# A SwiGLU block behind linear attention: the first chunk's output product by seven half-block products, one batch's projections and scores two slots later, and the closing additions in another order

## The chip, the cores and the metric

One core of one Trainium2 chip. The metric is the device time of one execution in microseconds (us). Time before: a median of 554.39 us over three runs, 553.97 to 556.33.

## What is computed

For each of 8 batches and 8 heads, keys and values of 1024 rows are first projected to 64 rows by E and F; the attention over these 64 rows gives 8192 rows of 512 numbers; a feed-forward block with gate and value weights of 512 x 1536 and output weights of 1536 x 512 follows.

```python
def _attn_ref(q, k, v, E, F):
    k_proj = np.einsum('ks,bhsd->bhkd', E, k)
    v_proj = np.einsum('ks,bhsd->bhkd', F, v)
    scale = 1.0 / np.sqrt(q.shape[-1])
    scores = scale * np.matmul(q, k_proj.transpose(0, 1, 3, 2))
    scores = scores - np.max(scores, axis=-1, keepdims=True)
    attn = np.exp(scores)
    attn = attn / (np.sum(attn, axis=-1, keepdims=True) + 1e-09)
    return np.matmul(attn, v_proj).astype(np.float32)

def _moe_ref(x, w_gate, w_val, w_out):
    g = x @ w_gate
    silu = g * (1.0 / (1.0 + np.exp(-g)))
    val = x @ w_val
    return (silu * val @ w_out).astype(np.float32)
```

## The kernel before

The 8192 rows are cut into 16 chunks of 512 rows, two for each batch: chunk c belongs to batch c // 2. The outer loop (L849 to L858) runs over 192 steps; step t does column tile f = t mod 12 (128 of the 1536) of chunk c = t // 12. In each step `f_g` (L471) makes the gate product, four TensorE products of 512 columns over the four tiles of 128 inputs, and a tanh on ACT (L474); `f_v` (L477) makes the value product in the same way, and DVE multiplies gate, tanh and value together in two instructions (L481 and L486) into `hT`, the chunk's hidden values. Gate and value have two PSUM banks each.

The attention of later batches is placed by hand in between. A step has two slots: slot 2t lies between the gate and the value product, slot 2t + 1 at the end. `place` (L651) says in which slot each piece of a batch runs: `u_KV` (projections of keys and values), `u_KT` (the projected keys turned, and copied into the block-diagonal tile BD by four DVE copies), `u_TD` (queries turned by a DMA transpose on the SP queue, tile qTd), `u_S` (scores, eight groups, with an exp on ACT), `u_R` (row sums and reciprocals on DVE, the softmax pair), `u_N` (the normalised weights AA on POOL), `u_AD` (AA turned by a DMA transpose on SP, tile AT), `u_PV` (the attention's output, tile xT, which the gate and value products read). Batch 0's own second chunk is attended to in slots 12 to 22 (L803 to L812), with transposes on TensorE. Loads of k, v and q go out from POOL's queue, in slots of their own (L817 to L823). Batches are counted from 0: the third batch is b = 2.

The output product of a chunk runs one chunk later, from the list `late` (L829 to L847), which is worked off in each step between the value product and slot 2t + 1. There are two ways of doing it:

- Chunk 0 before: `f_y` (L492), the plain product. Twelve parts of four 512-column products each; for each 128 rows one PSUM bank, one ACT copy (L507) and one store (L508).
- Chunks 1 to 15: `f_m` (L604), one level of a seven-product scheme. Rows, columns and inner length are halved, and seven products of half size stand for eight. Their operands are sums of quarters: of the weights once (`w_sum`, L517, five sums ws1, ws3, ws4, ws6, ws7 on DVE), of the hidden values for each chunk (`h_sum`, L530: hs5 and hs2 tile by tile on POOL, hs1, hs6 and hs7 whole on DVE). Each product is six 256-column TensorE products (`m_mm`, L554), for each of two halves p of 128 rows: 14 groups for a chunk, in the order 3, 4, 5, 2, 1, 6, 7. Products 3 and 4 lie in a bank "y", are copied by ACT and added on POOL (`m_34`); products 5 and 2 are then added on top in the same bank and copied (`m_52`); products 1 and 6 lie in a bank "z". `m_16` (L590) adds product 1 on DVE (L593) and subtracts on POOL (L594); product 7 is then added on top of product 1 in its half bank, and `m_7` (L596) makes the last add on DVE (L599) and stores (L600) from SP.

Small products of the attention take banks of the kind "a" (two), and in the first two chunks also the bank "z" as a third in turn (`ring["wide"]`, L143 and L851). The tiles of hs5, hs2, hs1, hs6, hs7 also hold the first batch's turned queries and its weights AA (`first_batch`, L308).

The last chunk has its output product at the end (`f_m_last`, L616): the seven products, and for each p three DVE additions (L633 to L635) that make two partial sums; then product 7 and product 1 are made in one half bank, each followed by a DVE add (L640) and a store (L641) from SP or ACT's queue. Product 1 is added on top of product 7, so it must wait for product 7's L640.

The instructions of every engine run in the order in which the program gives them.

Of the kernel before, what the change touches and what calls it, by code (L numbers as in the profile page):

```python
# [10 lines left out]
ALU = mybir.AluOpType  # L11
AX = mybir.AxisListType
BF16 = mybir.dt.bfloat16
FP32 = mybir.dt.float32
# [6 lines left out]
DM = H * D  # L21
DFF = 1536
P = 128
# [3 lines left out]
NFT = DFF // P  # L27
# [3 lines left out]
NC = B * CH  # L31
# [7 lines left out]
def kernel(  # L39
# [19 lines left out]
    nc = tc.nc  # L59
# [10 lines left out]
    y_pool = ctx.enter_context(tc.tile_pool(name="ysb", bufs=2))  # L70
# [18 lines left out]
    wo = w_pool.tile([P, NFT, DM], BF16, name="wo")  # L89
    ws = {m: w_pool.tile([P, HF, HC], BF16, name=f"ws{m}") for m in (1, 3, 4, 6, 7)}  # L90

    kb, vb, qb, xT, hT = {}, {}, {}, {}, {}
# [47 lines left out]
    ring = {"n": 0, "wide": True}  # L140

    def bank(where, shape, dt, name):
        if where == "a" and ring["wide"]:  # L143
            where = "aaz"[ring["n"] % 3]
            ring["n"] += 1
        pool, tag = banks[where]
        return pool.tile(shape, dt, name=name, tag=tag)
# [323 lines left out]
    def f_g(c, f, i=None):  # L471
        ps = f_mm(c, f, 0, i)
        th = fw.tile([P, CW], FP32, name="th", tag="th")
        nc.scalar.activation(out=th[:], in_=ps[:], func=AF.Tanh, scale=0.5)  # L474
        gp[0] = (ps, th)
# [11 lines left out]
            out=hT[c][:, f, :], in0=s1[:], scalar=0.5, in1=ps[:], op0=ALU.mult, op1=ALU.mult  # L487
        )

    yy = {}  # L490

    def f_y(c, n):  # L492

        i, part = divmod(n, 3)
        if part == 0:
            yy[c] = bank("y", [P, DM], FP32, "yps")
        for f in range(4 * part, 4 * part + 4):
            nc.tensor.matmul(
                out=yy[c][:],
                lhsT=hT[c][:, f, i * P : (i + 1) * P],  # L500
                rhs=wo[:, f, :],
                start=(f == 0),
                stop=(f == NFT - 1),
            )
        if part == 2:
            ysb = y_pool.tile([P, 2, DM], FP32, name="ysb", tag="ysb")
            nc.scalar.copy(out=ysb[:, 0], in_=yy[c][:])  # L507
            nc.sync.dma_start(out=rows_of(c)[:, i, :], in_=ysb[:, 0])  # L508

    def rows_of(c):  # L510
        b, ch = divmod(c, CH)
        return out[b * S : (b + 1) * S, :].rearrange("(p c j) d -> p c j d", c=CH, j=4)[:, ch]
# [41 lines left out]
    def m_mm(c, p, m, ps, start=False):  # L554

        for f in range(HF):
            if m == 3:
                lhsT = hT[c][:, f, p * P : (p + 1) * P]
            elif m == 4:
                lhsT = hT[c][:, HF + f, HT + p * P : HT + (p + 1) * P]  # L560
            else:
                lhsT = hs[c, m][:, f, p * P : (p + 1) * P]
            rhs = {2: wo[:, f, 0:HC], 5: wo[:, HF + f, HC:DM]}.get(m)
            nc.tensor.matmul(  # L564
                out=ps,
                lhsT=lhsT,
                rhs=ws[m][:, f, :] if rhs is None else rhs,
                start=(start and f == 0),
                stop=(f == HF - 1),
                skip_group_check=True,  # L570
            )

    xx, zz, tt, yo = {}, {}, {}, {}

    def m_bank(at):
        return bank(at, [P, 2, HC], FP32, "yps")

    def m_34(c, p):

        xs = d_pool.tile([P, 2, HC], FP32, name="xs", tag="d")  # L580
        nc.scalar.copy(out=xs[:], in_=xx[c, p][:])  # L581
        t = tt[c, p] = d_pool.tile([P, 2, HC], FP32, name="tt", tag="t")
        nc.gpsimd.tensor_tensor(out=t[:, 0], in0=xs[:, 0], in1=xs[:, 1], op=ALU.add)  # L583

    def m_52(c, p):

        ysb = yo[c, p] = y_pool.tile([P, 4, HC], FP32, name="ysb", tag="ysb")
        nc.scalar.copy(out=ysb[:, 1:3], in_=xx.pop((c, p))[:])  # L588
# [27 lines left out]
    def f_m_last(c):  # L616

        xx[c, 0], xx[c, 1] = m_bank("y"), m_bank("g")
        z6 = m_bank("a")
        z1 = [m_bank("av"[p]) for p in range(2)]  # L620
        for p in range(2):
            m_mm(c, p, 3, xx[c, p][:, 0], start=True)
        for p in range(2):
            m_mm(c, p, 6, z6[:, p], start=(p == 0))
        for p in range(2):
            m_mm(c, p, 4, xx[c, p][:, 1])
            m_34(c, p)
        for p in range(2):
            m_mm(c, p, 5, xx[c, p][:, 0])
            m_mm(c, p, 2, xx[c, p][:, 1])  # L630
            m_52(c, p)
            d, ysb = tt[c, p], yo[c, p]
            nc.vector.tensor_tensor(out=d[:, 1], in0=d[:, 0], in1=ysb[:, 2], op=ALU.subtract)  # L633
            nc.vector.tensor_tensor(out=d[:, 0], in0=d[:, 0], in1=ysb[:, 1], op=ALU.subtract)
            nc.vector.tensor_tensor(out=d[:, 1], in0=d[:, 1], in1=z6[:, p], op=ALU.add)  # L635
        for x in (1, 0):
            for p in range(2):
                m_mm(c, p, (7, 1)[x], z1[p][:, 0], start=(x == 1))
                ysb = yo[c, p]
                nc.vector.tensor_tensor(out=ysb[:, 3 * x], in0=tt[c, p][:, x], in1=z1[p][:, 0], op=ALU.add)  # L640
                (nc.sync, nc.scalar)[p].dma_start(  # L641
                    out=rows_of(c)[:, p + 2 * x, :], in_=ysb[:, 2 * x : 2 * x + 2].rearrange("p x d -> p (x d)")
                )


    slots = defaultdict(list)

    def put(s, fn, *a):
        slots[s].append((fn, a))

    def place(b):  # L651
        s0 = 48 * (b - 1)
        if b == 1:
            put(22, u_TD, 1, 0)
            put(29, u_K1, 1)
            put(32, u_KT, 1)
            put(40, u_V1, 1)
            sa = (35, 36, 37, 38, 41, 42, 43, 44)
            put(41, u_AD, 1, 0)
            put(30, u_TD, 1, 1)  # L660
            put(47, u_AD, 1, 1)
            sp = (44, 45, 46, 46, 66, 67, 68, 69)
        else:
            put(s0 + (8 if b == 2 else 0), u_KV, b)
            put(s0 + (11 if b == 2 else 3), u_KT, b)
            o = 14 if b == 2 else 6
            put(s0 + (9 if b == 2 else -6), u_TD, b, 0)
            put(s0 + (11 if b == 2 else -4), u_TD, b, 1)
            sa = [s0 + o + 3 * j for j in range(NJ)]
            put(sa[3] + 4, u_AD, b, 0)  # L670
            put(sa[7] + 4, u_AD, b, 1)
            sp = [s0 + i for i in (39, 41, 43, 45, 57, 59, 61, 63)]
        for j in range(NJ):
            put(sa[j], u_S, b, j)
            put(sa[j] + 1, u_R, b, j)
            put(sa[j] + 1, u_N, b, j)
        for i in range(8):
            put(sp[i], u_PV, b, i // 4, i % 4)

    def run_slot(s):  # L680
        for fn, a in slots.pop(s, ()):
            fn(*a)

    with tc.manual_schedule():
# [3 lines left out]
        for i in range(2):  # L688
            nc.scalar.dma_start(
                out=kraw[i][:],  # L690
                in_=k[0, 2 * i : 2 * i + 2].rearrange("h (p j) d -> p h (j d)", j=NJ),
# [123 lines left out]
        for b in range(1, B):  # L815
            place(b)
        for b in range(2, B):  # L817
            s0 = 48 * (b - 1) - (20 if b == 3 else 24)
# [8 lines left out]


        late = defaultdict(list)  # L829
        for n in range(NFT):  # L830
            late[NFT + 4 + (2 * n + 1) // 3].append((f_y, 0, n))
        for m, f in ((3, 6), (4, 7), (6, 8), (7, 9), (1, 10)):
            late[NFT + f].append((w_sum, m))
        for c in range(1, NC):
            for f in range(HF):
                for m in (5, 2):
                    late[c * NFT + HF + f].append((h_sum, c, m, f, f + 1))
            if c == NC - 1:
                late[c * NFT + HF].append((h_sum, c, 6, 0, HF, nc.vector))
                for f in (0, 2, 4):  # L840
                    for m in (1, 7):
                        late[c * NFT + HF + f + 1].append((h_sum, c, m, f, f + 2, nc.vector))
            else:
                for i, m in enumerate((1, 6, 7)):
                    late[(c + 1) * NFT + 1 + i].append((h_sum, c, m, 0, HF, nc.vector))
                for n, f in enumerate((0, 1, 2, 3, 4, 4, 5, 6, 7, 8, 9, 10, 10, 11)):
                    late[(c + 1) * NFT + f].append((f_m, c, n))  # L847

        for t in range(NIT):  # L849
            c, f = divmod(t, NFT)  # L850
            ring["wide"] = c < 2  # L851
            i = 1 if t < 2 else None
            f_g(c, f, i)
            run_slot(2 * t)
            f_v(c, f, i)
            for fn, *a in late.pop(t, ()):
                fn(*a)
            run_slot(2 * t + 1)  # L858
        f_m_last(NC - 1)
        assert not slots and not late  # L860

# [28 lines left out]
```

## Time and profile before

The profiled execution took 554.06 us; its span from first to last instruction is 552.3 us at a granted TensorE clock of 1.000. The profile gives, for a line of the program, the busy time, the mean length of one instruction, and the idle time of its engine before it with what ended that. Some groups that matter here:

| line | engine | what | count | mean ns |
|---|---|---|---|---|
| L474 | ACT | tanh of the gate | 191 | 598 |
| L481 | DVE | gate times tanh | 191 | 676 |
| L486 | DVE | times value, into hT | 192 | 688 |
| L547 | POOL | h_sum of one tile | 180 | 691 |
| L547 | DVE | h_sum, whole | 49 | 946 |
| L383 | POOL | AA | 56 | 1043 |
| L583 | POOL | add of m_34 | 30 | 981 |
| L594 | POOL | subtraction of m_16 | 28 | 1268 |
| L368 | DVE | row sums | 64 | 677 |
| L357 | ACT | exp | 64 | 598 |

Loads of 512 KB of q take 18.1 us from issue to landing (median), of 1 MB of v 14.8, the two halves of the output weights wo 19.4 and 23.3; a DMA transpose of queries 6.0, of AA 4.2; a store of 512 KB 2.7.

Busy times of engines say little by themselves: an engine that isn't the bound may idle at no cost. What counts is where TensorE waits, and what ended that wait. A time of a merged row of several products is from the first start to the last end, and ends overlap with the next start; the pace is read from start to start.

### The profile page before, as it was taken

The page shows a single profiled execution, that of the slowest core. Times are in us where ns is not written, and L with a number is a line of the kernel's source. Part 1 is how long each engine was busy: PE and PEld are TensorE (multiplying, and loading weights), DVE is VectorE, ACT ScalarE, POOL GpSimd, SP SyncE. Part 2 cuts the span into 40 slices and gives each one's busy share as a digit, 9 for nine tenths or more (in the row PEclk, how much of TensorE's full clock was granted, in tenths as well). Part 3 has the DMA queues.
Part 4 walks back from the last instruction along what each step waited for, and adds up shares of the span by engine and source line. Part 5 has one row for each costly group of instructions (what it writes and reads, how often), then busy time and mean ns, then how long its engine had stood idle before and what let it go on. Part 6 is the DMA issues. An engine that isn't in the chain of part 4 may idle for free. (4 is left out here: it accounts for less than half of the span.)

```text
span 552.3 us, 9270 instructions
## 1 busy us (share of the span) xinstructions
PE 537.3 (97%) x3438; PEld 317.9 (58%) x3500; DVE 414.1 (75%) x699; ACT 233.3 (42%) x416; POOL 294.5 (53%) x364
## 2 busy tenths in 40 slices
PE   7999999999999999999999999999999999999996
PEld 4654545566565655566556655566656565555565
DVE  3787896878597875979579785788859786676883
ACT  3564453353445333443425434344244533433331
POOL 7851493467617934377534855268461763526171
PEclk9999999999999999999999999999999999999999
DMA  9999969929932598038941299214990212110013
GB/s 205 192 197 190 162 142 194 160 72 139 211 76 73 104 189 170 1 77 145 206 108 39 64 170 195 71 39 92 179 209 17 74 47 72 39 40 31 8 39 115
DMA packets 111630, 62.87 MB, mean 114 GB/s; under 512 B 65888, under 2 KB 102752, under 8 KB 111584
## 3 DMA queue, kind: packets, MB, share of 16 engines
q0 software_dynamic: 43952, 29.49, 37.5%
q1 hardware_dynamic: 66800, 31.20, 25.4%
q10 hardware_dynamic: 832, 1.57, 0.9%
q8 instruction: 27, 0.44, 0.3%
q14 instruction: 19, 0.16, 0.1%
HBM read 60.29 MB, written 16.78 MB: 140 GB/s over the span
## 5 line engine op out<-in xcount | busy, mean ns | idle before, releaser
L462 PE MATMUL vps<-xT,wv 128*128 128x512 bf16 (+1 forms) x759 | 195.0, 377 | 2.5 <-DMA wv<-in_moe_w_val_dram 0.8
L462 PE MATMUL gps<-xT,wg 128*128 128x512 bf16 (+1 forms) x729 | 191.6, 377 | 1.9
L474 ACT ACTIVATE th<-gps 128x512 f32<-128x512 f32 x191 | 114.1, 598 | 164.7 <-PE gps L462 153.9
L481 DVE SCALAR_TENSOR_TENSOR s<-th,gps 128x512 f32<-128x512 f32 x191 | 129.2, 676 | 67.5 <-ACT th L474 66.2
L547 POOL TENSOR_TENSOR hs<-hT 128x256 bf16<-128x256 bf16 x180 | 120.6, 691 | 57.9 <-DVE hT L486 57.2
L486 DVE SCALAR_TENSOR_TENSOR hT<-s,vps 128x512 bf16<-128x512 f32 x192 | 132.1, 688 | 20.4 <-PE gps L462 0.5
L462 PEld LDWEIGHTS <-wv 128*128 128x128 bf16 x776 | 73.9, 98 | 84.3 <-issue 3.0
L564 PEld LDWEIGHTS <-hs 128*128 128x128 bf16 x900 | 88.0, 98 | 36.7 <-issue 3.3
L462 PEld LDWEIGHTS <-wg 128*128 128x128 bf16 x776 | 74.1, 98 | 55.9 <-issue 0.6
L383 POOL TENSOR_TENSOR AAd<-ee,rr 128x512 bf16<-128x512 f32 x56 | 58.4, 1043 | 55.7 <-issue 33.6
L594 POOL TENSOR_TENSOR tt<-tt,ysb 128x512 f32<-128x512 f32 x28 | 35.5, 1268 | 71.7 <-DVE tt L593 71.7
L564 PE MATMUL yps<-ws,hs 128*128 128x256 bf16 x540 | 68.6, 272 | 1.5 <-DVE ysb L640 1.2
L583 POOL TENSOR_TENSOR tt<-xs 128x256 f32<-128x256 f32 x30 | 29.4, 981 | 51.3 <-ACT xs L581 51.2
L150 ACT CAST xT<-pv 128x512 bf16<-128x512 f32 (+1 forms) x63 | 36.4, 581 | 46.3 <-PE pv L410 44.3
L368 DVE TENSOR_REDUCE zz<-ee 128x8 f32<-128x512 f32 x64 | 43.3, 677 | 11.1 <-ACT ee L357 11.0
L564 PE MATMUL yps<-ws,hT 128*128 128x256 bf16 x360 | 48.8, 273 | 0.0
L564 PE MATMUL yps<-wo,hs 128*128 128x256 bf16 x360 | 48.6, 273 | 0.1
L547 DVE TENSOR_TENSOR hs<-hT 128x1536 bf16<-128x1536 bf16 (+1 forms) x49 | 46.1, 946 | 0.1
L357 ACT ACTIVATE ee<-sc 128x512 f32<-128x512 f32 x64 | 38.1, 598 | 18.5 <-PE sc L353 16.1
L564 PEld LDWEIGHTS <-hT 128*128 128x128 bf16 x360 | 35.2, 98 | 16.0
L581 ACT COPY xs<-yps 128x512 f32<-128x512 f32 x30 | 17.6, 585 | 30.6 <-PE yps L564 30.5
L588 ACT COPY ysb<-yps 128x512 f32<-128x512 f32 x30 | 17.6, 585 | 24.9 <-PE yps L564 21.6
(100 smaller groups left out, 318.0 us busy)
## 6 DMA issues: line engine op xcount, KB each, us to landing
out_dram<-ysb SPq DMA_DIRECT2D x28, 512.0 KB, 2.7
qb<-in_q_dram POOLq DMA_DIRECT2D x14, 512.0 KB, 18.1
kb<-in_k_dram POOLq DMA_DIRECT2D x7, 1024.0 KB, 9.9
vb<-in_v_dram POOLq DMA_DIRECT2D x7, 1024.0 KB, 14.8
wo<-in_moe_w_out_dram POOLq DMA_DIRECT2D x2, 768.0 KB, 21.4
out_dram<-ysb SPq DMA_DIRECT2D x6, 256.0 KB, 2.2
kraw<-in_k_dram ACTq DMA_DIRECT2D x2, 512.0 KB, 4.8
qb<-in_q_dram POOLq DMA_DIRECT2D x4, 256.0 KB, 7.9
```

What stands on the lines that cost most here:

```text
L150: (nc.scalar.copy if eng is nc.scalar else eng.tensor_copy)(out=out, in_=in_)
L357: nc.scalar.activation(out=e[:].rearrange("p h j k -> p (h j k)"), in_=ps[:].rearrange("p a k -> p (a k)"), func=AF.Exp, scale=scale,)
L368: nc.vector.reduce_sum(out=z[:], in_=e[:], axis=AX.X)
L383: eng.tensor_tensor(out=a.rearrange("p j h k -> p h j k"), in0=ee.pop((b, u))[:], in1=rr.pop((b, u))[:].unsqueeze(3).to_broadcast([P, 4, 2 ...
L462: nc.tensor.matmul(out=ps[:, ts], lhsT=(wg, wv)[w][:, kt, f * P : (f + 1) * P], rhs=x[:, kt, ts], start=(kt == 0), stop=(kt == NKT - 1),)
L474: nc.scalar.activation(out=th[:], in_=ps[:], func=AF.Tanh, scale=0.5)
L481: nc.vector.scalar_tensor_tensor(out=s1[:], in0=th[:], scalar=1.0, in1=g[:], op0=ALU.add, op1=ALU.mult)
L486: nc.vector.scalar_tensor_tensor(out=hT[c][:, f, :], in0=s1[:], scalar=0.5, in1=ps[:], op0=ALU.mult, op1=ALU.mult)
L547: eng.tensor_tensor(out=hs[c, m][:, fs, :], in0=quarter(hT[c], *a)[:, fs], in1=quarter(hT[c], *b)[:, fs], op=op,)
L564: nc.tensor.matmul(out=ps, lhsT=lhsT, rhs=ws[m][:, f, :] if rhs is None else rhs, start=(start and f == 0), stop=(f == HF - 1), skip_group ...
L583: nc.gpsimd.tensor_tensor(out=t[:, 0], in0=xs[:, 0], in1=xs[:, 1], op=ALU.add)
L594: nc.gpsimd.tensor_tensor(out=t[:], in0=t[:], in1=yo[c, p][:, 1:3], op=ALU.subtract)
```

## The change

Chunk 0's output product is made by `f_m` as that of the others. `f_y` goes. Its h_sums are made in steps 6 to 11 (hs5, hs2, POOL) and 13 to 15 (hs1, hs6, hs7, DVE), the weight sums ws3 and ws4 in step 16, ws1 in 17, ws6 and ws7 in 18, and its 14 product groups stand in steps 17 to 23, three of them (1, 6 and 7) in step 19. The bank "z" is given to the attention only until step 16. Batch 2's projections, turned keys, queries, scores and what hangs on them stand two slots (one step) later. In the last chunk, product 6 is added to the partial sum before products 5 and 2, and the subtractions are ordered so that those of the lower half p = 1 come last; one of them stands after product 7's adds.

```diff
-    def f_y(c, n):
...
-        for f in range(4 * part, 4 * part + 4):
-            nc.tensor.matmul(
-                out=yy[c][:],
-                lhsT=hT[c][:, f, i * P : (i + 1) * P],
-                rhs=wo[:, f, :],
...
+        add, sub = ALU.add, ALU.subtract
+
+        def step(o, i0, i1, op):
+            nc.vector.tensor_tensor(out=o, in0=i0, in1=i1, op=op)
+
+        for p in range(2):
+            step(tt[c, p][:, 1], tt[c, p][:, 0], z6[:, p], add)
         for p in range(2):
             m_mm(c, p, 5, xx[c, p][:, 0])
             m_mm(c, p, 2, xx[c, p][:, 1])
             m_52(c, p)
-            d, ysb = tt[c, p], yo[c, p]
-            nc.vector.tensor_tensor(out=d[:, 1], in0=d[:, 0], in1=ysb[:, 2], op=ALU.subtract)
-            nc.vector.tensor_tensor(out=d[:, 0], in0=d[:, 0], in1=ysb[:, 1], op=ALU.subtract)
-            nc.vector.tensor_tensor(out=d[:, 1], in0=d[:, 1], in1=z6[:, p], op=ALU.add)
+        d, ysb = [tt[c, p] for p in range(2)], [yo[c, p] for p in range(2)]
+        step(d[0][:, 1], d[0][:, 1], ysb[0][:, 2], sub)
+        step(d[0][:, 0], d[0][:, 0], ysb[0][:, 1], sub)
+        step(d[1][:, 1], d[1][:, 1], ysb[1][:, 2], sub)
         for x in (1, 0):
             for p in range(2):
                 m_mm(c, p, (7, 1)[x], z1[p][:, 0], start=(x == 1))
-                ysb = yo[c, p]
-                nc.vector.tensor_tensor(out=ysb[:, 3 * x], in0=tt[c, p][:, x], in1=z1[p][:, 0], op=ALU.add)
+                step(ysb[p][:, 3 * x], d[p][:, x], z1[p][:, 0], add)
...
+            if x:
+                step(d[1][:, 0], d[1][:, 0], ysb[1][:, 1], sub)
...
-            put(s0 + (8 if b == 2 else 0), u_KV, b)
-            put(s0 + (11 if b == 2 else 3), u_KT, b)
-            o = 14 if b == 2 else 6
-            put(s0 + (9 if b == 2 else -6), u_TD, b, 0)
-            put(s0 + (11 if b == 2 else -4), u_TD, b, 1)
+            put(s0 + (10 if b == 2 else 0), u_KV, b)
+            put(s0 + (13 if b == 2 else 3), u_KT, b)
+            o = 16 if b == 2 else 6
+            put(s0 + (11 if b == 2 else -6), u_TD, b, 0)
+            put(s0 + (13 if b == 2 else -4), u_TD, b, 1)
...
-        for n in range(NFT):
-            late[NFT + 4 + (2 * n + 1) // 3].append((f_y, 0, n))
-        for m, f in ((3, 6), (4, 7), (6, 8), (7, 9), (1, 10)):
+        for m, f in ((3, 4), (4, 4), (1, 5), (6, 6), (7, 6)):
             late[NFT + f].append((w_sum, m))
-        for c in range(1, NC):
+        for c in range(NC):
...
-                for n, f in enumerate((0, 1, 2, 3, 4, 4, 5, 6, 7, 8, 9, 10, 10, 11)):
+                fs = (5, 5, 6, 6, 7, 7, 7, 8, 8, 9, 9, 10, 10, 11) if c == 0 else (0, 1, 2, 3, 4, 4, 5, 6, 7, 8, 9, 10, 10, 11)
+                for n, f in enumerate(fs):
                     late[(c + 1) * NFT + f].append((f_m, c, n))
...
-            ring["wide"] = c < 2
+            ring["wide"] = t < NFT + 5
```

More of the change, by code (lines that the diff above doesn't have):

```diff
@@ L488, in f_v @@
         )
-    yy = {}
-    def f_y(c, n):
-        i, part = divmod(n, 3)
-        if part == 0:
-            yy[c] = bank("y", [P, DM], FP32, "yps")
-        for f in range(4 * part, 4 * part + 4):
-            nc.tensor.matmul(
-                out=yy[c][:],
-                lhsT=hT[c][:, f, i * P : (i + 1) * P],
-                rhs=wo[:, f, :],
[L502 to L508, printed above, removed]
     def rows_of(c):
@@ L638, in f_m_last @@
                 m_mm(c, p, (7, 1)[x], z1[p][:, 0], start=(x == 1))
-                ysb = yo[c, p]
-                nc.vector.tensor_tensor(out=ysb[:, 3 * x], in0=tt[c, p][:, x], in1=z1[p][:, 0], op=ALU.add)
+                step(ysb[p][:, 3 * x], d[p][:, x], z1[p][:, 0], add)
                 (nc.sync, nc.scalar)[p].dma_start(
-                    out=rows_of(c)[:, p + 2 * x, :], in_=ysb[:, 2 * x : 2 * x + 2].rearrange("p x d -> p (x d)")
+                    out=rows_of(c)[:, p + 2 * x, :], in_=ysb[p][:, 2 * x : 2 * x + 2].rearrange("p x d -> p (x d)")
                 )
+            if x:
+                step(d[1][:, 0], d[1][:, 0], ysb[1][:, 1], sub)
     slots = defaultdict(list)
```

## The prediction

> **What bounds the kernel now.** I read the busy table first (us, share of the span, instructions), then what TensorE (PE) waited for (us in total, times, longest), then the order of time around the change on PE and DVE, then the end.
>
> ```profile
> PE 537.3 (97%) x3438; PEld 317.9 (58%) x3500; DVE 414.1 (75%) x699; ACT 233.3 (42%) x416; POOL 294.5 (53%) x364
> ```
>
> ```profile
> PE yps L564 <- DVE ysb L640: 1.2, 1, 1.2
> PE kvp L162 <- DMA vb<-in_v_dram: 0.9, 1, 0.9
> ...
> PE sc L353 <- DMA qTd<-qb: 0.4, 1, 0.4
> ```
>
> TensorE is busy 97%: a product less is time won, a wait of TensorE is time lost. The waits are few; one lies at the end (L640), one at the third batch's projections (vb), one at its first scores (qTd). Next, TensorE around the first chunk's output product (start us, length us, what, count), and one later half-block product:
>
> ```profile
> 55.38 1.03 PE L498 MATMUL yps<-wo,hT 128*128 128x512 bf16 x4
> 56.24 1.03 PE L462 MATMUL gps<-xT,wg 128*128 128x512 bf16 x4
> 57.10 1.03 PE L462 MATMUL vps<-xT,wv 128*128 128x512 bf16 x4
> 57.97 1.89 PE L498 MATMUL yps<-wo,hT 128*128 128x512 bf16 x8
> 59.70 0.39 PE L353 MATMUL sc<-BD,qTd 128*128 128x128 bf16 x4
> ...
> 83.30 0.82 PE L564 MATMUL yps<-ws,hT 128*128 128x256 bf16 x6
> 83.96 1.03 PE L462 MATMUL gps<-xT,wg 128*128 128x512 bf16 x4
> ```
>
> From start to start, four 512-column products take 0.86 us and six 256-column ones 0.66 us. Then DVE in the same place:
>
> ```profile
> 54.30 0.69 DVE L486 SCALAR_TENSOR_TENSOR hT<-s,vps 128x512 bf16<-128x512 f32 x1
> 54.90 0.41 DVE L275 CAST BD<-kTp 64x256 bf16<-64x256 f32 x1
> ...
> 56.68 0.69 DVE L481 SCALAR_TENSOR_TENSOR s<-th,gps 128x512 f32<-128x512 f32 x1
> 57.47 0.69 DVE L486 SCALAR_TENSOR_TENSOR hT<-s,vps 128x512 bf16<-128x512 f32 x1
> ...
> 63.27 0.95 DVE L526 TENSOR_TENSOR ws<-wo 128x1536 bf16<-128x1536 bf16 x1
> 64.14 0.68 DVE L368 TENSOR_REDUCE zz<-ee 128x8 f32<-128x512 f32 x1
> ```
>
> and the busy time of the engines in three stretches (steps 12 to 15, 16 and 17, 18 to 23):
>
> ```profile
> 45.53:53.54 8.01, 7.96 (x48) 3.83 (x48) 5.47 (x10) 2.76 (x5) 0.00 (x0) 1.00 1.21 196
> 53.54:59.70 6.16, 6.16 (x32) 2.86 (x31) 5.61 (x10) 1.19 (x2) 0.00 (x0) 1.00 1.27 177
> 59.70:81.58 21.88, 21.72 (x135) 11.12 (x137) 19.17 (x34) 11.52 (x21) 17.68 (x19) 1.00 0.75 141
> ```
>
> After the stretch's length come PE, PEld, DVE, ACT and POOL, each with its count. DVE's is 5.61 of 6.16 us and 19.17 of 21.88: it is nearly full exactly where the change gives it more.
>
> **Part 1, the product itself.** Removed: 12 groups of four 512-column products, 12 × 0.86 = 10.37 us. Added: 14 groups of six, 14 × 0.656 = 9.18. TensorE gains **1.19 us**. Four ACT copies (0.59) become four of the same size: nothing. DVE gets three h_sums of 0.95 (rows of 87.05 to 91.81), two adds of 0.41 (L593) and two of 0.68 (L599): 5.0 us. POOL gets 12 h_sums, two adds of 0.98 and two of 1.27.
>
> **DVE becomes late at step 17.** I go along DVE by starts, with pitches from rows: a 128x1536 sum 0.87 (63.27 to 64.14), L481 to L486 0.79, L486 to the next 0.60. Before, hT of step 13 began at 49.74. Now: h_sum 1 at 50.34; L481 of step 14 at 51.21 (before 50.68), L486 52.00; h_sum 6 at 52.60; L481 of step 15 at 53.51 as before (1.35 us of idle there swallow it), L486 54.30; h_sum 7 at 54.90; so the four casts 54.90 to 56.68 move to 55.77; L481 and L486 of step 16 at 57.55 and 58.34; the sum for product 3 at 58.94, ended 59.89; the one for product 4 at 59.81, ended 60.76. wo has landed (33.59 + at most 23.3 = 56.9). TensorE has no output product in step 16 now: its step 17 begins at 55.38 and asks for product 3 at 57.10. It waits 57.10 to 59.9, then 0.2 for the next sum: **+3.0 us**. Behind it in TensorE's queue stand the first scores of batch 1.
>
> **And again at step 19.** Product 7 adds to the half bank that m_16's DVE add must have read (the changed program carries this wait), and products 1, 6, 7 stand in one step without a gate product between. After product 4 (61.4) TensorE has four score groups of 0.22, two gate and two value products (0.86 each), and products 5, 2, 1, 6 (2.62): 6.94 us, so it stands at product 7 at 68.4. DVE from 60.68: L481+L486 1.39, sum 1 0.87, softmax pair 0.90 (64.14 to 65.04), 1.35, sums 6 and 7 1.74, two pairs 1.75, 1.35, the add 0.41 = 9.76, so 70.4. Wait 2.1 us at least. A sum took 1.24 and 1.84 us beside POOL (67.24, 78.63), so up to 0.9 more; of five sums three took 0.95, I take **+2.4** (2.1 to 3.0). Behind product 7 stands step 20. DVE's next, L599, waits for POOL's 1.27 us, and behind that the fourth softmax pair, the BDV casts and step 20's L481; two banks each for gate and value leave a step of room, and AT's transpose (4.2 us to landing, asked for at some 74.4, used at 80) still has 1 us.
>
> **POOL earlier, steps 6 to 11.** A pair of h_sums took 1.29 us (81.48) and 1.94 beside a DVE sum (63.43); no such sum runs here, so 1.29. After hT of step 6 (34.54) the queue is: pair, AA (1.04), pair (from 37.2), AA, AA, pair, AA, which ends the second AA at 39.5 and the fourth at 42.9. TensorE transposes them at 39.45 and 43.15. Cost 0.1, taken as nothing; with 1.94 it is 1.3. Loads of vb and qb behind them go out 1.9 us later and are used late enough (67.6 and 70.3 before).
>
> **Two banks instead of three** for "a" from step 17: a score bank is free after exp (0.60); steps there are over 3 us. Nothing; at most one exp, 0.6, if ACT is behind.
>
> **Part 2, batch 2 two slots later.** Moved: 16 projection matmuls with 3 copies, 4 turns with 4 casts, 8 score groups with exp, softmax pair and AA, and two qTd and two AT transposes. On SP the first qTd transpose now stands behind one output store of chunk 1; the others pass none. The loads aren't moved. At the projections the first K product ran at 92.06 and the next at 93.33, where a pair's pitch is 0.215: 1.05 lost. One step later is 2.4 us, and the 5.4 us of waits above delay TensorE more than the vb load (behind step 21's h_sums on POOL, some 4 us later): **-1.05** (0 to -1.05). The qTd wait at 103.65: **-0.4** (0 to -0.4), by the same.
>
> **Part 3, the end.**
>
> ```profile
> 544.27 0.58 ACT L588 COPY ysb<-yps 128x512 f32<-128x512 f32 x1 [0.72 <-PE yps L564]
> ...
> 545.14 0.42 DVE L633 TENSOR_TENSOR tt<-tt,ysb 128x256 f32<-128x256 f32 x1
> ...
> 546.26 0.75 DVE L640 TENSOR_TENSOR ysb<-tt,yps 128x256 f32<-128x256 f32 x2
> 546.73 1.47 PE L564 MATMUL yps<-ws,hs 128*128 128x256 bf16 x12 [1.18 <-DVE ysb L640]
> ```
>
> After the second copy (544.85) three DVE operations stood before the first L640; now one does, the z6 adds go where DVE idled 3.97 us. L640 starts at 545.3 (copy to use 0.03, as at 50.65) to 545.75 (0.45, as at 544.00) instead of 546.26: **-0.7** (-0.5 to -0.95). The subtraction placed between lies under the 0.66 us of product 1.
>
> **Sum.** -1.19 + 3.0 + 2.4 - 1.05 - 0.4 - 0.7 = **+2.1 us**. The profiled execution took 554.06 (span 552.3, 1.76 around it): 556.2. The median shown is 554.39, 0.33 above it: **556.5**. The ends: 3.0 + 2.1 - 1.19 - 1.05 - 0.4 - 0.95 = +1.5 and 3.0 + 3.0 + 0.6 - 1.19 - 0.5 = +4.9, so 555.9 to 559.3 for this case.
>
> [...]
>
> **Rivals.** *DVE is not late:* both waits fall away. For it: DVE idles 1.46 us at 59.55. Against: that idle lies behind the place. Sum -3.3; but scores then come at 58.4 and qTd landed at 59.5 (40.69 + 18.8): +1.1 unless it lands sooner. 552.2, or 551.0. If only step 19's wait falls away, 554.1. *POOL's queue is the bound (slower):* pairs take 1.94, so the fourth AA comes at 44.4 and TensorE waits 1.3 us at its transpose before step 12: 557.8. It decides from 1.5 us a pair. For it: 180 h_sums average 691 ns, above 645; against: no DVE sum runs beside. *The order doesn't do what it says:* projections still wait for vb since POOL asks for it behind more work: +1.05, 557.5.
>
> **Chances.** Forecast 0.55 (likeliest part 555.9 to 558), DVE not late, in part or whole, 0.20, POOL 0.15, vb 0.10. A measurement of this kernel tells about 0.5% (2.8 us) from no change: 551.6 and 557.2 are the bounds. Faster: half of the second case, 0.10. Slower: the last two and 0.08 of the forecast, 0.33. Same: the rest, 0.57. The range reaches from above the case without waits to near the forecast's upper end: 552.8 to 558.8.
>
> **What would show it.** TensorE waiting for the sums ws on DVE for some 3 us near 57, and for m_16's add for some 2 us a step or two later; no wait for vb; the last wait on DVE 0.5 us or less. Wrong if TensorE stays unbroken from 45 to 85 us, or if waits appear at AA's transposes near 43.

## The result, and the profile after

The changed kernel takes a median of 560.43 us over six runs (559.40 to 562.94) against 554.35 for the kernel before: a ratio of 1.0109, 95% interval 1.0081 to 1.0137. It is slower by about 1.1%. The forecast was 556.5 us: the sign of its sum was right, the size was not, and the time lies outside the range given (552.8 to 558.8). The profiled execution took 559.89 us, with a span of 558.1 (before 552.3) and a granted clock of 0.997 (before 1.000).

TensorE's waits after (us in total, times, longest). Behind the place where `f_y` stood, the lines of the changed kernel have numbers 19 lower: `w_sum`'s L526 is L507, `m_mm`'s L564 is L545, the adds of `m_16` and `m_7` are L574 and L580, the store is L581.

```profile
PE sc L353 <- DMA qTd<-qb: 2.8, 1, 2.8
PE yps L545 <- DVE ws L507: 2.7, 1, 2.7
PE yps L545 <- DVE tt L574: 1.8, 1, 1.8
```

The two waits on DVE are those that the prediction named: the weight sum for product 3, and m_16's add ahead of product 7. The wait for vb is gone, and so is that on the last DVE adds. The wait for qTd, which was to vanish, has grown from 0.4 to 2.8. TensorE in order of time (start us, length us, what, count, and in brackets the idle time before and its releaser):

```profile
56.46 1.03 PE L462 MATMUL vps<-xT,wv 128*128 128x512 bf16 x4
60.15 2.72 PE L545 MATMUL yps<-ws,hT 128*128 128x256 bf16 x12 [2.66 <-DVE ws L507]
62.66 0.63 PE L353 MATMUL sc<-BD,qTd 128*128 128x128 bf16 x4
63.09 1.27 PE L462 MATMUL gps<-xT,wg 128*128 128x512 bf16 x4
64.20 0.39 PE L353 MATMUL sc<-BD,qTd 128*128 128x128 bf16 x4
...
68.77 1.47 PE L545 MATMUL yps<-ws,hs 128*128 128x256 bf16 x12
72.07 0.81 PE L545 MATMUL yps<-ws,hs 128*128 128x256 bf16 x6 [1.83 <-DVE tt L574]
...
112.65 0.40 PE L353 MATMUL sc<-BD,qTd 128*128 128x128 bf16 x4 [2.76 <-DMA qTd<-qb]
```

The reader is to see three breaks, at 60.15, 72.07 and 112.65, and something behind the first that no list of waits shows. From 60.15 to the second score group at 64.20 lie 12 products of 256 columns, four score products and a gate product: at the pitches of the rest of the trace 1.31 + 0.22 + 0.86 = 2.39 us. They took 4.05. The stretches of the trace say why (length; PE, PEld, DVE, ACT, POOL busy with counts; granted clock, DMA share, GB/s):

```profile
58.00:60.00 2.00, 0.00 (x0) 0.00 (x0) 1.90 (x3) 0.00 (x0) 0.00 (x0) 1.00 1.24 200
60.00:62.00 2.00, 1.85 (x9) 1.32 (x9) 1.90 (x4) 0.00 (x0) 0.00 (x0) 0.54 1.32 203
62.00:64.00 2.00, 2.00 (x13) 1.28 (x11) 1.22 (x2) 1.08 (x2) 0.43 (x1) 0.61 1.33 182
64.00:66.00 2.00, 1.95 (x16) 1.34 (x16) 1.76 (x4) 1.08 (x2) 1.20 (x2) 1.00 0.09 12
...
72.00:74.00 2.00, 1.88 (x15) 1.20 (x17) 0.62 (x3) 0.22 (x1) 1.91 (x3) 1.00 0.03 8
...
112.00:116.00 4.00, 3.29 (x21) 1.99 (x23) 1.49 (x3) 1.13 (x3) 1.38 (x4) 1.00 0.63 141
```

After the idle stretch of 2.66 us TensorE ran at half its clock (0.50 from 61 to 63 us). A mean of 0.54 over 2 us is 1.84 us at one half, 0.61 is 1.56: 3.4 us together, during which 1.7 us of work is lost. Not all of it is added time: in experiment 2 below, whose profile has a clock of 1.00 here, the same stretch takes 2.61 us (59.57 to 62.18), because product 4 waits 0.2 us for its own sum. So of the 1.66 us too much, 0.2 is that sum and 1.4 the clock. After the second break, 1.83 us of idle, the clock is 1.00 (72 to 74), and after the third, which with 2.76 us is as long as the first, too (112 to 116). DVE in the same places:

```profile
55.12 0.95 DVE L528 TENSOR_TENSOR hs<-hT 128x1536 bf16<-128x1536 bf16 x1
...
59.14 1.82 DVE L507 TENSOR_TENSOR ws<-wo 128x1536 bf16<-128x1536 bf16 x2
...
71.60 0.41 DVE L574 TENSOR_TENSOR tt<-tt,yps 128x256 f32<-128x256 f32 x1
...
99.92 0.42 DVE L574 TENSOR_TENSOR tt<-tt,yps 128x256 f32<-128x256 f32 x1
103.21 0.43 DVE L174 CAST BDV<-kvp 64x256 bf16<-64x256 f32 x1 [2.86 <-ACT ks L170]
103.65 0.43 DVE L175 CAST BDV<-kvp 64x256 bf16<-64x256 f32 x1
...
105.49 0.68 DVE L580 TENSOR_TENSOR ysb<-tt,yps 128x512 f32<-128x512 f32 x1
```

The last four belong to the third break. The projections were moved into the step of product 7, so DVE now waits 2.86 us for their copy on ACT (L170) between m_16's add (L574) and m_7's (L580). The store needs L580, and the transpose stands behind the store, as SP's queue shows:

```profile
106.23 0.37 SPq L581 DMA_DIRECT2D out_dram<-ysb  x1
106.78 6.43 SPq L331 DMA_TRANSPOSE qTd<-qb  x2
```

Before, that transpose was issued ahead of the store:

```profile
97.69 3.89 SPq L331 DMA_TRANSPOSE qTd<-qb  x1
101.69 0.52 SPq L600 DMA_DIRECT2D out_dram<-ysb  x1
```

What SP waited for ahead of the store in the changed kernel:

```profile
SPq L581 <- DVE ysb L580: 7.4, 1, 7.4
```

The end, on DVE:

```profile
551.56 0.42 DVE L612 TENSOR_TENSOR tt<-tt,ysb 128x256 f32<-128x256 f32 x1 [0.55 <-ACT ysb L569]
551.90 0.77 DVE L612 TENSOR_TENSOR ysb<-tt,yps 128x256 f32<-128x256 f32 x2
```

One subtraction stands between the second copy (ended 551.53) and the first of product 7's adds: 0.37 us, where it was 1.41.

The span's 5.8 us by terms, each the difference of the two traces in its place:

| term | predicted us | measured us |
|---|---|---|
| seven products instead of eight | -1.19 | -1.19 |
| steps 6 to 11 (start of step 12: 45.53, now 45.75) | 0 | +0.2 |
| waits for the sums at products 3 (57.32 to 60.15) and 4 (0.22) | +3.0 | +3.05 |
| half clock behind them (4.05 for 2.61) | 0 | +1.4 |
| wait at product 7 (70.08 to 72.07) | +2.4 | +2.0 |
| wait for vb | -1.05 | -1.05 |
| first scores of batch 2 (0.57 lost before, 2.92 after) | -0.4 | +2.35 |
| the end | -0.7 | -1.0 |
| sum | +2.1 | +5.8 |

The product's term is the prediction's own arithmetic; the start of step 24 bears it out: it went from 81.58 to 87.09 us, +5.51, where the first five terms give 0.22 + 3.05 + 1.44 + 1.99 - 1.19 = 5.51.

### The profile page after: what moved, and what is told of

The parts are those of the page before. It is cut to its first block, busy times and chain, and to the rows that moved or that the text cites. A ratio compares the mean times of both kernels' runs of the same rounds, so it can differ in the third digit from the quotient of the medians.

```text
span 558.1 us, 9360 instructions
## 1 busy us (share of the span) xinstructions
PE 539.0 (97%) x3474; PEld 322.1 (58%) x3536; DVE 418.8 (75%) x706; ACT 232.9 (42%) x416; POOL 305.4 (55%) x380
## 4 chain that ended last, share of the span: by engine, by line
PE 79%; DVE 12%; DMA 3%; issue 2%; POOL 1%; ACT 1%; DVEq 0%; POOLq 0%; ACTq 0%
PE gps L462 25%; PE vps L462 24%; PE yps L545 23%; DVE s L481 3%; DVE hs L528 3%; DVE hT L486 2%; DMA wv<-in_moe_w_val_dram 2%; PE pv L410 2%; PE kvp L162 2%; PE sc L353 2%; DMA qTd<-qb 1%; DVE BD L276 1%; DVE BD L275 1%; ACT th L474 1%; DVE zz L368 1%
## 5 line engine op out<-in xcount | busy, mean ns | idle before, releaser
L462 PE MATMUL gps<-xT,wg 128*128 128x512 bf16 (+1 forms) x737 | 194.9, 377 | 1.8
L528 POOL TENSOR_TENSOR hs<-hT 128x256 bf16<-128x256 bf16 x192 | 127.2, 685 | 62.8 <-DVE hT L486 62.0
L545 PEld LDWEIGHTS <-hs 128*128 128x128 bf16 x960 | 93.8, 98 | 39.5 <-issue 4.2
L545 PE MATMUL yps<-ws,hs 128*128 128x256 bf16 x576 | 73.2, 272 | 2.5 <-DVE tt L574 1.8
L575 POOL TENSOR_TENSOR tt<-tt,ysb 128x512 f32<-128x512 f32 x30 | 38.1, 1269 | 64.9 <-DVE tt L574 63.7
L564 POOL TENSOR_TENSOR tt<-xs 128x256 f32<-128x256 f32 x32 | 31.0, 969 | 64.7 <-ACT xs L562 64.4
L545 PE MATMUL yps<-ws,hT 128*128 128x256 bf16 x384 | 53.0, 277 | 3.2 <-DVE ws L507 2.7
L545 PE MATMUL yps<-wo,hs 128*128 128x256 bf16 x384 | 51.5, 273 | 0.2
L545 PEld LDWEIGHTS <-hT 128*128 128x128 bf16 x384 | 38.1, 99 | 20.1 <-issue 2.9
L528 DVE TENSOR_TENSOR hs<-hT 128x1536 bf16<-128x1536 bf16 (+1 forms) x52 | 49.0, 947 | 0.1
```

The source lines that it names most:

```text
L462: nc.tensor.matmul(out=ps[:, ts], lhsT=(wg, wv)[w][:, kt, f * P : (f + 1) * P], rhs=x[:, kt, ts], start=(kt == 0), stop=(kt == NKT - 1),)
L528: eng.tensor_tensor(out=hs[c, m][:, fs, :], in0=quarter(hT[c], *a)[:, fs], in1=quarter(hT[c], *b)[:, fs], op=op,)
L545: nc.tensor.matmul(out=ps, lhsT=lhsT, rhs=ws[m][:, f, :] if rhs is None else rhs, start=(start and f == 0), stop=(f == HF - 1), skip_group ...
L575: nc.gpsimd.tensor_tensor(out=t[:], in0=t[:], in1=yo[c, p][:, 1:3], op=ALU.subtract)
```

## The experiments

Times are medians; ratios are against the kernel before, run beside it on the same chip (554.13 to 554.37 us there).

**1. The transpose ahead of the store again.** Of the changed kernel, one line is undone.

```diff
-            put(s0 + (11 if b == 2 else -6), u_TD, b, 0)
+            put(s0 + (9 if b == 2 else -6), u_TD, b, 0)
```

> The changed kernel with one transpose of batch 2's queries (the first, qTd of chunk 0) put back to slot 57, ahead of chunk 1's output store on SP. Theory: in the changed kernel SP waits 7.4 us in front of that store for DVE's last add, and the transpose stands behind it, so TensorE waits 2.76 us for qTd at the first scores. Expected: that wait is gone or under 0.5 us, 2.3 to 2.8 us less than the changed kernel (some 557.9 where that has 560.4). Rival: the load of q sets the time, as the profile of before said; then the wait stays over 2 us and the time is the same.

Measured: 558.25 us, ratio 1.0068 (1.0053 to 1.0084), span 556.6. SP's queue and TensorE's wait:

```profile
104.80 3.44 SPq L331 DMA_TRANSPOSE qTd<-qb  x1
108.34 0.52 SPq L581 DMA_DIRECT2D out_dram<-ysb  x1
```

```profile
PE sc L353 <- DMA qTd<-qb: 1.2, 1, 1.2
```

The wait shrinks from 2.8 to 1.2, and the span by 1.5. So 1.6 us is the store's place on SP. What is left has another cause. The transpose waits for q's load, as it did before (5.6 us, before 6.6), but that load went out later (at 84.71 in the changed kernel, 79.52 before), and so the transpose goes out 7.1 us later than before (104.80 against 97.69), while TensorE comes to these scores only 6.8 us later (109.87 against 103.08). Each theory holds for a part.

**2. TensorE kept busy during the first wait.** Twelve products of numbers that nobody reads stand ahead of product 3.

```diff
+        def keep_busy(n):
+            ps = bank("z", [P, CW], FP32, "warm")
+            for _ in range(n):
+                nc.tensor.matmul(
+                    out=ps[:], lhsT=wg[:, 0, 0:P], rhs=wg[:, 0, 0:CW],
+                    start=True, stop=True,
+                )
...
+            if t == NFT + 5:
+                keep_busy(12)
```

> The changed kernel with 12 products of 512 columns put before product 3 of chunk 0, of numbers that nobody reads, in a bank that is free there (12 x 0.216 = 2.6 us in a wait of 2.7). Theory: the wait for the weight sums stays, but TensorE isn't idle in it, so its clock stays at 1.00, where the changed kernel's profile shows 0.50 to 0.71 from 60.1 to 64 us. Expected: granted clock 1.000 and 1.4 to 1.8 us less than the changed kernel. Rival: the clock fell for another reason than the idle stretch (the second wait near 70 us didn't lower it); then it falls here too and the time is the same or longer.

Measured: 559.62 us, ratio 1.0105 (1.0069 to 1.0142), span 557.5. TensorE and its clock:

```profile
56.76 2.75 PE L841 MATMUL warm<-wg 128*128 128x512 bf16 x12
59.57 1.68 PE L545 MATMUL yps<-ws,hT 128*128 128x256 bf16 x12
...
70.38 1.43 PE L545 MATMUL yps<-ws,hs 128*128 128x256 bf16 x6 [2.16 <-DVE tt L574]
```

```profile
60.00:62.00 2.00, 1.89 (x17) 1.33 (x16) 1.90 (x4) 0.71 (x2) 0.05 (x1) 1.00 1.31 204
...
70.00:72.00 2.00, 1.43 (x6) 1.00 (x7) 0.41 (x2) 0.00 (x0) 1.65 (x3) 0.61 0.03 8
72.00:74.00 2.00, 1.98 (x11) 0.80 (x12) 1.40 (x3) 0.45 (x1) 1.34 (x3) 0.54 0.19 72
```

With the gap filled, the clock stays at 1.00 from 60 to 70 us, as it should if the idle stretch, and not the work behind it, lowers the clock. One profile doesn't show that by itself, for in experiment 3 the clock stays up with the gap left idle. The traces together speak for it: in those of the kernels before and after between 20 us and the last products, and in the stretches of experiments 2, 3, 5 and 7 whose clock is known, it falls only in or behind an idle stretch of TensorE of 2.16 us or more. Here it falls after the second wait, which is 2.16 us, and stays down 3.4 us again (0.61 and 0.54 in two stretches of 2 us). The median is only 0.8 us below the changed kernel's, where 1.4 to 1.8 was expected. By the spans, which leave out that two of the four runs took 2.3 and 2.9 us around them instead of 1.8, it is 1.7 less (557.0 against 558.7); with runs spread over 5 us neither number decides, only the windows show the clock.

**3. Product 7 a step later.**

```diff
-                fs = (5, 5, 6, 6, 7, 7, 7, 8, 8, 9, 9, 10, 10, 11) if c == 0 else (0, 1, 2, 3, 4, 4, 5, 6, 7, 8, 9, 10, 10, 11)
+                fs = (5, 5, 6, 6, 7, 7, 8, 8, 8, 9, 9, 10, 10, 11) if c == 0 else (0, 1, 2, 3, 4, 4, 5, 6, 7, 8, 9, 10, 10, 11)
```

> The changed kernel with product 7 of the first half of chunk 0 in step 20 instead of 19. Theory: its wait for m_16's add on DVE (1.83 us) falls under the gate, value and projection products of step 20; 1.8 to 2.0 us less than the changed kernel, first wait and clock unchanged. Rival: DVE is late as a whole, so TensorE only waits elsewhere in steps 19 to 22, and less than 0.5 us is won.

Measured: 558.53 us, ratio 1.0081 (1.0059 to 1.0104), span 556.2. The waits:

```profile
PE yps L545 <- DVE ws L507: 2.7, 1, 2.7
PE sc L353 <- DMA qTd<-qb: 2.3, 1, 2.3
PE pv L410 <- DMA AT<-AAd: 1.9, 1, 1.9
```

The wait at product 7 is gone, and a wait of the same size for AT has taken its place. That is the rival's outcome, TensorE only waits elsewhere. AA's last piece on POOL and the transpose that makes AT of it:

```profile
73.43 1.04 POOL L383 TENSOR_TENSOR AAd<-ee,rr 128x512 bf16<-128x512 f32 x1
75.13 3.35 SPq L338 DMA_TRANSPOSE AT<-AAd  x1
```

AA is complete at 74.47. Chunk 0's store (74.61) holds the transpose back by 0.7 us at most, and it lands after 5.1 us instead of the changed kernel's 4.2. So AT is there at 80.2, where the changed kernel has it at 80.3; but TensorE comes for it at 78.4 instead of 81.7. In the changed kernel the wait at product 7 and the half clock had hidden this one.

The median is 1.9 us below the changed kernel's, which is the theory's number, but not for the theory's reason. In the profiles 0.5 us of it is a shorter wait for qTd, and the other 1.4 lie ahead of step 24 (85.68 against 87.09), where the wait only moved and the clock did not fall after the first wait:

```profile
60.00:62.00 2.00, 1.83 (x17) 1.49 (x17) 1.90 (x4) 0.16 (x1) 0.00 (x0) 1.00 1.28 203
```

That the number came out is luck. An idle stretch of the same length, 2.7 us, lowered the clock in the changed kernel's profile and not in this one. Runs of one program differ too: this experiment's four have mean clocks of 0.998, 0.998, 0.995 and 0.994.

**4. Part 3 alone, on the kernel before:** the closing order, as in the diff of the change.

> The kernel before with the closing additions in the new order alone. Theory: it is worth what the changed kernel's end shows (the wait of product 1 for DVE falls from 1.18 to 0.15 us): 0.9 to 1.0 us less than before, 553.4. Rival: the stores or the last additions end the span as late as before; then under 0.3 us.

Measured: 553.05 us, ratio 0.9982 (0.9973 to 0.9991), span 551.2: 1.1 us less than before. The part is worth what the trace of the whole change showed, 1.0.

**5. Part 2 alone, on the kernel before** (products and end as before).

```diff
-            put(s0 + (8 if b == 2 else 0), u_KV, b)
-            put(s0 + (11 if b == 2 else 3), u_KT, b)
-            o = 14 if b == 2 else 6
-            put(s0 + (9 if b == 2 else -6), u_TD, b, 0)
-            put(s0 + (11 if b == 2 else -4), u_TD, b, 1)
+            put(s0 + (10 if b == 2 else 0), u_KV, b)
+            put(s0 + (13 if b == 2 else 3), u_KT, b)
+            o = 16 if b == 2 else 6
+            put(s0 + (11 if b == 2 else -6), u_TD, b, 0)
+            put(s0 + (13 if b == 2 else -4), u_TD, b, 1)
```

> The kernel before with batch 2 two slots later alone, the transposes of queries too. By the forecast's step both waits at batch 2 go: 1.05 + 0.4 = 1.4 us less than before. By what the changed kernel shows, the first transpose stands behind chunk 1's store here too: the vb wait goes (-1.05), and the wait at the first scores grows from 0.4 to 1 to 3 us, so between 1 us less and 1.5 us more than before.

Measured: 556.71 us, ratio 1.0033 (1.0023 to 1.0044), span 555.5. The wait for vb is gone, and that for qTd is there without any seven products for chunk 0:

```profile
101.17 0.39 SPq L600 DMA_DIRECT2D out_dram<-ysb  x1
101.67 5.87 SPq L331 DMA_TRANSPOSE qTd<-qb  x2
```

```profile
107.23 0.58 PE L353 MATMUL sc<-BD,qTd 128*128 128x128 bf16 x4 [2.40 <-DMA qTd<-qb]
```

Part 2 was to gain 1.45 us and costs 2.3 by the medians (556.71 against 554.37). In the profiled run, too, the clock fell behind the wait of 2.4 us, to 0.50 from 108 to 110 us. The ten runs fall into two groups: four of 555.15 to 555.22 us with a mean clock of 0.999 or 1.000, and six of 556.62 to 557.25 with 0.996 or 0.997. So one and the same program goes either way, and the half clock costs some 1.6 us where it comes; without it part 2 costs 0.8.

**6. Parts 2 and 3 with the first transpose left where it was,** on the kernel before: as 4 and 5, but `u_TD` of the first half stays at `s0 + 9`.

> The kernel before with the new closing order and with batch 2 two slots later, but with its first transpose of queries left in slot 57, ahead of chunk 1's store. Theory: the vb wait (1.05) and the qTd wait (0.4) both go, with no wait behind the store, and the end gives 1.0: 2.4 us less than before, 551.9, clock 1.000. Rival: the load of q isn't there in time even so; then a wait of 1 us or more stays at the first scores, and the gain is 1 to 1.5.

Measured: 551.49 us, ratio 0.9953 (0.9938 to 0.9968), span 549.8. Of batch 2 one wait is left:

```profile
PE sc L353 <- DMA qTd<-qb: 0.2, 1, 0.2
```

Part 2 is good once this one transpose is not moved with it: by the medians 5.2 us separate this run from experiment 5, of which 1.1 is part 3 and the other 4.1 this line (the wait of 2.4, and the half clock after it in the runs that have it).

**7. The seven products with the sums wanted last.** Of the changed kernel, with the transpose at `s0 + 9`: chunk 0's products run in the order 2, 5, 3, 4, 1, 6, 7, since 2 and 5 need no weight sum; the five sums are made one step apart, in steps 17 to 21; a function `f_m0` holds the products in banks y and z so that product 7 stands a step or more behind m_16's add; the first score piece is one slot later.

```diff
...
-        for m, f in ((3, 4), (4, 4), (1, 5), (6, 6), (7, 6)):
+        for m, f in ((3, 5), (4, 6), (1, 7), (6, 8), (7, 9)):
...
+                for f, p, m in ((4, 0, 2), (5, 0, 5), (5, 1, 2), (6, 1, 5), (6, 0, 3), (7, 0, 4), (7, 1, 3),
+                                (8, 1, 4), (8, 0, 1), (9, 0, 6), (9, 1, 1), (10, 1, 6), (10, 0, 7), (11, 1, 7)):
+                    late[NFT + f].append((f_m0, p, m))
...
```

> The changed kernel with chunk 0's products in another order: 2 and 5 of both halves first, which need no weight sums, so that each of the five sums can be made one step apart in steps 17 to 21; product 7 of each half a step or more behind its product 6; the first scores of batch 1 one slot later; batch 2's first transpose of queries in slot 57. The two halves use the two banks y and z, and the partial sums are formed the other way round. Theory: the waits for sums and for m_16 were a matter of order, not of DVE's total; they go, the clock stays at 1.00, and 1.2 + 1.0 + 1.0 us are won against before: 551 to 552. Rival: DVE has no room for the 5 us of work more in these steps in any order; then TensorE waits 2 us or more elsewhere in steps 17 to 23 and the time is over 553.

Measured: 557.32 us, ratio 1.0046 (1.0023 to 1.0068), span 556.5. Both waits on DVE are gone and step 24 starts at 81.41, 0.17 before the old 81.58. The time is not the 551 to 552 that was expected, for:

```profile
PE kvp L162 <- DMA vb<-in_v_dram: 4.0, 1, 4.0
```

```profile
98.00:100.00 2.00, 0.37 (x2) 0.18 (x3) 0.00 (x0) 0.00 (x0) 0.00 (x0) 0.57 1.49 140
100.00:102.00 2.00, 2.00 (x12) 1.13 (x10) 0.00 (x0) 0.00 (x0) 0.00 (x0) 0.50 1.34 184
102.00:104.00 2.00, 2.00 (x8) 0.49 (x5) 0.15 (x1) 0.58 (x1) 0.00 (x0) 0.50 1.44 187
104.00:106.00 2.00, 2.00 (x11) 1.14 (x10) 1.87 (x4) 0.00 (x0) 0.00 (x0) 0.73 1.68 173
```

POOL, with the h_sums and subtractions of the new products ahead, asks for vb at 79.60 instead of 77.64, and TensorE no longer comes late enough to hide that. The prediction's last rival (projections wait for vb behind POOL's work) was hidden in the changed kernel only by its other waits. The clock here stays at one half for 1.72 + 2 + 2 + 1.08 = 6.8 us, twice 3.4. Two of the six runs kept a mean clock of 1.000, and took 554.88 and 555.41 us.

**8. Batch 2's loads much earlier,** on the kernel of experiment 4.

```diff
-            at = (43, 43, 44, 45) if b == 2 else (s0, s0 + 2, s0 + 4, s0 + 6)
+            at = (36, 41, 37, 42) if b == 2 else (s0, s0 + 2, s0 + 4, s0 + 6)
```

> The kernel before with the new closing order, and batch 2 where it was, but its loads asked for earlier (slots 36, 41, 37, 42 instead of 43, 43, 44, 45). Theory: the waits at batch 2 came from loads that were asked for late; both go, 2.4 us less than before, 551.9. Rival: the transfers share the DMA engines with batch 1's (busy 99% to 64 us); then batch 1's transposes or loads are late and the gain is under 1.2.

Measured: 569.29 us (560.12 to 571.27); with this spread only the sign is read. The waits, in a run of 568.83 us:

```profile
PE sc L353 <- DMA qTd<-qb: 7.5, 1, 7.5
PE pv L410 <- DMA AT<-AAd: 6.9, 1, 6.9
```

The rival holds: with nothing but the loads moved, batch 1's DMA transposes come late. TensorE waits 7.46 us for qTd, until 77.97; before, the same scores start at 70.32 without a wait, as their transpose lands 4.2 us after its issue at 65.17. Even the shortest of the four runs is 6 us longer than the kernel before, far more than the vb wait was worth; how long it waited for the transposes isn't recorded.

**9. Batch 2 four slots later still,** on experiment 7 (the first transpose unmoved).

```diff
-            put(s0 + (10 if b == 2 else 0), u_KV, b)
-            put(s0 + (13 if b == 2 else 3), u_KT, b)
-            o = 16 if b == 2 else 6
+            put(s0 + (14 if b == 2 else 0), u_KV, b)
+            put(s0 + (17 if b == 2 else 3), u_KT, b)
+            o = 20 if b == 2 else 6
...
-            put(s0 + (13 if b == 2 else -4), u_TD, b, 1)
+            put(s0 + (15 if b == 2 else -4), u_TD, b, 1)
```

> The other order of chunk 0's products (as in e7_order), with batch 2's projections and scores four slots later still. Theory: nothing is left in that order but the wait of 4.0 us for batch 2's vb, whose load is issued behind POOL's added work and landed at 99.6 us; two steps are 4.8 us, so the wait goes, the clock stays up, and 1.2 + 1.0 + 1.0 + 0.4 are won against before: 550.7. Rival: the piece of batch 2 that is pressed now (AA's transposes, the third chunk pair's weights) is late for its attention output at step 43 and a wait comes there.

Measured: 561.56 us, ratio 1.0132 (1.0115 to 1.0149), span 560.8. No wait for vb, and in its place:

```profile
PE pv L410 <- DMA AT<-AAd: 7.8, 2, 7.5
```

Later isn't safer: TensorE stands still for 7.55 us, until AT is there at 144.32. What held AA's transpose back is not shown.

**10. The loads one slot earlier,** on experiment 7.

```diff
-            at = (43, 43, 44, 45) if b == 2 else (s0, s0 + 2, s0 + 4, s0 + 6)
+            at = (42, 42, 43, 44) if b == 2 else (s0, s0 + 2, s0 + 4, s0 + 6)
```

> As e7_order, with batch 2's four loads one slot earlier (42, 42, 43, 44). Theory: they go out some 5 us earlier on POOL, ahead of m_16's subtraction, and the wait for vb (4.0) falls under 1 us: 552 to 553. Rival: they then run beside AA's DMA transpose of batch 1 (used at 76 us), as in e8_loads, and TensorE waits for AT instead: no gain, or a loss.

Measured: 551.52 us, ratio 0.9956 (0.9940 to 0.9973), span 549.3. The wait for vb is gone; of the waits of the attention only a small one is new:

```profile
PE pv L410 <- DMA AT<-AAd: 0.5, 1, 0.5
```

**11. and 12. The two good versions side by side:** experiment 6 (eight products for chunk 0) and experiment 10 (seven).

> The kernel of e6_later_td_end (plain product for chunk 0, parts 2 and 3 with the transpose ahead of the store) beside e12_seven on one chip. Both theories expect 551.5.

> The kernel of e10_loads42 (seven products for chunk 0 in the other order, loads a slot earlier) beside e11_plain. Theory: TensorE's 1.19 us less work shows once no wait is left, so 0.5 to 1.2 us less than e11_plain; its one remaining wait of its own is 0.5 at AT. Rival: what the seven products save goes into small waits in any order; then the two differ by less than 0.3 us.

Measured: 551.79 us, ratio 0.9963 (0.9953 to 0.9973), and 551.07 us, ratio 0.9944 (0.9932 to 0.9956). The second is the best version, 3.1 us under the kernel before. The two medians differ by 0.7 us, but the intervals overlap a little, and in the two profiles the stretch from step 12 to step 24 shrinks by less than the 1.19 us that the products save: 36.04 us (45.62 to 81.66) in experiment 11, 35.57 (45.82 to 81.39) in experiment 12. The 0.72 us missing are lost again at two DMA transposes that come late. At AT it is 0.43 from start to start, of which the trace shows 0.26 as idle:

```profile
75.97 0.39 PE L410 MATMUL pv<-AT,BDV 128*128 128x512 bf16 x1 [0.26 <-DMA AT<-AAd]
```

The other 0.28 stand ahead of a score group of batch 1 at 70.74, whose weights waited for qTd. So parts 2 and 3, mended, are worth 2.4 us, and the seven products 0.5 more by these two profiles and 0.7 by the medians, with intervals that overlap.

## Why the prediction was right or wrong

- *The product itself, -1.19:* right by the start of step 24 in the changed kernel; in experiment 12, with the waits on DVE gone, 0.5 of it is left, since two transposes that come late take 0.7.
- *DVE late at step 17, +3.0:* right in place, cause and size. Product 3 waited for ws3 from 57.32 to 60.15, 2.8 us, and the second sum adds 0.2. The walk along DVE had put the sum at 58.94, it began at 59.14.
- *Nothing behind that wait:* wrong. Neither the sum nor its upper end has a term for TensorE's clock. The wait was 2.66 us by the trace and TensorE ran at half clock for 3.4 us behind it, which cost 1.4 us. Nor is that cost certain: experiment 5, with a wait of 2.4 us in its profile, has the lower mean clock in six runs of ten.
- *Product 7 behind m_16's add, +2.4:* right in place and cause, 2.0. TensorE came 1.7 us later than worked out (70.08 against 68.4), 1.4 for the clock and the rest for a later product 3, and DVE 1.3 later (72.07 against 70.8); the wait is the difference. AT had its "1 us" in hand (there at 80.3, used at 81.68), but only because of the waits: experiment 3 shows that without this one TensorE loses the same 1.9 us at AT.
- *POOL in steps 6 to 11, 0:* near enough, +0.2; the rival of 1.3 us there is refuted.
- *vb, -1.05:* right, and for the reason given: TensorE came late. Experiment 7 shows the other side: with the waits taken away, vb is missing for 4.0 us. The moved slot alone is enough with the plain product for chunk 0 (experiment 5), not with the seven products' work on POOL.
- *qTd, -0.4:* the step that failed most, by 2.75 us: it measured +2.35. The prediction wrote that "the first qTd transpose now stands behind one output store of chunk 1" and gave that no price. The store waited 7.4 us on SP for its data, and the transpose behind it in SP's queue waited with it. The store was late because DVE's m_7 add stood behind the moved projections' copy. Experiment 1 puts 1.6 us on this, and experiment 5 shows it without the products. The rest is q's load. The prediction let this wait vanish "by the same" as the one for vb: TensorE delayed more than a load that goes out "some 4 us later". q's load went out 5.2 us later, and by experiment 1 its transpose can go out 7.1 us later and TensorE comes 6.8 later, so nothing is gained on it.
- *The end, -0.7:* right in kind; -1.0 by the trace and -1.1 in experiment 4, past the sum's best case of -0.95, as the remaining subtraction took 0.34 us of pitch and nothing else stood between.

Two terms, 2.75 for qTd and 1.44 for the clock, make 4.19 us. The others are together 0.44 better than predicted: 2.06 + 4.19 - 0.44 = 5.81.

## What to carry to other kernels

A piece that is moved to a later slot is moved past everything on the queue that issues it: ask of each instruction passed when *its* data are ready, for here the transpose waited behind the store at the head of SP's queue, not for its own input alone (1.6 us by experiment 1). A wait of TensorE was charged twice here, once as idle (2.66 us) and once as half clock (1.4), so ask after each added wait of such a length, in these runs from 2.16 us, what the work behind it costs at half speed. Before judging that a saving doesn't pay, put the operations whose operands are late last: up to step 24 the same seven products cost 5.5 us in one order and nothing in another. Behind it, one transpose and some loads then had to stand a slot or two from where they had been.

## What the runs showed of the hardware that was not expected

TensorE's granted clock fell in or behind idle stretches of 2.16, 2.40, 2.66 and 4.0 us (experiment 2, experiment 5, the changed kernel, experiment 7). Behind 7.46 and 7.55 us (experiments 8 and 9) four 512-column products took 1.91 us, as they did at half clock behind the wait of experiment 5, where such a row takes 1.03 at a clock of 1.00. The clock did not fall behind 1.83 and 2.76 us in the changed kernel's own trace, 2.3 in experiment 2, or 2.7 and 2.26 in experiment 3. Where it fell behind less than 3 us it was one half for 3.4 us; in experiment 7 for twice that, 6.8. So from 2.16 to 2.76 us the length of the idle stretch alone did not decide, and a walk that prices such a wait at its idle time has a term of 0 or up to 1.7 us (half of 3.4) that it can't fix beforehand. The ten runs of experiment 5 show both outcomes in one program, and the six of the changed kernel fit that: 559.40 to 559.90 us at a mean clock of 0.997, 560.97 and 561.89 at 0.994, 562.94 at 0.989.

DMA transposes took far longer to land while bulk loads were under way. In the kernel before, the transpose of AT issued at 70.67 us took 4.2 us; the next one, issued at 84.76 behind batch 2's four loads (issued from 76.70 to 82.72, the last landing after 18.9 us), took 15.8. In experiments 8 and 9, which move these loads and batch 2's pieces, TensorE waited 6.9 to 7.55 us for transposes for which it had not waited before.
